# Weights of five attention groups of round two computed on VectorE during the first MoE

## The chip, the cores and the metric

One core of a Trainium2 chip runs the program. The metric is device time in microseconds (us) of one execution. The kernel before took 979.59 us, the median of three runs (979.09 to 980.57). Engines are written as in the profile: PE is TensorE (matrix products; PEld its loading of weights), DVE is VectorE, ACT is ScalarE, POOL is GpSimd, SP is SyncE; POOL and SP here issue transfers.

## The reference

An attention with pooled keys, whose output goes through a feed-forward layer (called MoE below). There are B = 4 batches with 12,288 queries each, C = 128 channels.

```python
kv_pool = kv.reshape(B, H // r, r, W // r, r, C).mean(axis=(2, 4))   # 768 keys a batch
kv_flat = kv_pool.reshape(B, -1, C) @ w_sr
k = v = kv_flat
s = scale * (q @ k.transpose(0, 2, 1))          # scale = 1 / sqrt(128)
a = np.exp(s - s.max(-1, keepdims=True))
a /= a.sum(-1, keepdims=True) + 1e-09
x = (a @ v).reshape(B * N, 128)
h = x @ w_in                                    # 128 -> 2048
g = h * (1.0 / (1.0 + np.exp(-1.702 * h)))
out = g @ w_out                                 # 2048 -> 128, fp32
```

The kernel takes the exponential without subtracting the maximum (the scores are small), and divides by the sum at the end.

## The kernel before

*Tiles.* The 49,152 queries are 96 groups of G = 512, 24 to a batch. For each group and each of JC = 6 chunks of 128 keys, TensorE makes a 128x512 tile of scores (L319), ScalarE its exponential into `ag` as bf16 (L321, three chunks an activation), and TensorE multiplies with the values: four query tiles of T = 128, for each a 128x129 product per chunk (L330); the 129th column of `v` is ones, so it is the sum. After three query tiles ("a unit") VectorE divides (L338, L346). In the MoE each group has FCH = 16 chunks: TensorE makes 128x512 of h (L433), ScalarE the activation into `ag` (L435), TensorE adds up the 16 products with w_out (L440), VectorE transposes the sum (L447), SP sends it out (L450).

*Rounds.* There are R = 2 rounds of 48 groups: attention of groups 0 to 47, MoE of 0 to 47, attention of 48 to 95, MoE of 48 to 95. `x` holds the attention output of one round. For the first 72 query tiles of a round it is turned on TensorE (`turn`, L356, L358), for the others by transfers through DRAM (L366, L372) during the MoE. Batches 2 and 3, which round two needs, are pooled during the first MoE: the sums by accumulating transfers (L161), then `use_kv`: sum on VectorE (L167), transposition (L172, L174), keys (L180, L181), values (L187, L189).

*Fills and drains.* A matmul that feeds an activation (L319, L433) is called a fill, one that uses its result (L330, L440) a drain. `ag` is one tile with AG = 108 slots of a chunk each. `place` gives slots out in a ring, `slot_of` says which are taken, `room_ahead` how many are free ahead. Drains may lag fills by as much as the ring holds.

*PSUM.* There are eight banks. Fills go to banks 0 to 2 and 3 to 5 in turn, three chunks each, and so a fill waits for the activation two before. Banks 6 and 7 are accumulators for all else (`acc`): the sum of a MoE group (`o_of`), a unit of the attention (`av_of`), a turn, the pooled keys. `closes` and `free` hold when the planner thinks an accumulator is free again.

*The order.* The scheduler of the language is off (`manual_schedule`); the order of instructions on each engine is the order of the Python calls. A loop over the activations (`seq`) plans it: it calls `fill(n + 2)`, then puts in whatever TensorE still has time for by the planner's clock, `now` for TensorE and `end` for ScalarE, in units of about one 512-column matmul: first a turn, then one of the `extras` (pooled keys), else the next drain in `todo`, as long as it ends before `limit`, or the ring is nearly full (`room`). Constants such as FIXED, CHUNK, COST and EVACUATE are the planner's estimates. Nothing in the plan keeps account of VectorE, but for fixed allowances. When a group first appears in `seq`, `background` or `background_moe` issues transfers for later groups: `load_qT` (SP, L200), `cast_q` (POOL, L195), `add_kv`, `put_away`, `bring_back`.

Of the kernel before, what the change touches and what calls it, by code (L numbers as in the profile page):

```python
# [6 lines left out]

F32 = mybir.dt.float32
F32R = mybir.dt.float32r
BF = mybir.dt.bfloat16  # L10
AF = mybir.ActivationFunctionType
AX = mybir.AxisListType
ADD = mybir.AluOpType.add
MUL = mybir.AluOpType.mult
GE = mybir.AluOpType.is_ge
LE = mybir.AluOpType.is_le
EQ = mybir.AluOpType.is_equal


@with_exitstack  # L20
def kernel(
    ctx, tc, q, kv, w_sr, moe_w_in, moe_w_out, out,
):
    nc = tc.nc
# [5 lines left out]
    JC = J // 128  # L30
    d_ff = moe_w_in.shape[1]
    FCH = d_ff // 128
    scale = 1.0 / (C ** 0.5)
# [20 lines left out]

    R = 2
    XS = NS // R
    AG = 108

    cpool = ctx.enter_context(tc.tile_pool(name="const", bufs=1))
    xpool = ctx.enter_context(tc.tile_pool(name="x", bufs=1))  # L60
# [122 lines left out]
    def make_v(b, a):  # L183
        ps = acc()
        pT = pTs.pop((b, a))
        for k in range(K):
            nc.tensor.matmul(ps[:, k * C:(k + 1) * C], pT[:, k * 128:(k + 1) * 128], w_sr_sb,  # L187
                             start=True, stop=True)
        nc.vector.tensor_copy(vs[b][:, a * K:(a + 1) * K, 0:C], ps[:, :h].rearrange("p (k c) -> p k c", k=K))  # L189

    qTs = {}

# [90 lines left out]


    slot_of = {}
    head = 8 * JC

    def place(chunks):
        nonlocal head
        if chunks[0][0] == "a" and chunks[0][1] < 8:  # L290

            lo = [i * JC + jc for _, i, jc in chunks]
            slot_of.update(zip(chunks, lo))
            return ag[:, lo[0]:lo[-1] + 1:JC, :]
        if head + len(chunks) > AG:
            head = 0
        lo = head
        head += len(chunks)
        busy = set(slot_of.values())
        for c in chunks:  # L300
            assert lo not in busy
            slot_of[c] = lo
            lo += 1
        return ag[:, head - len(chunks):head, :]

    def room_ahead():
        busy = set(slot_of.values())
        return next((n for n in range(AG) if (head + n) % AG in busy), AG)

    def weights(c):  # L310
        return ag[:, slot_of[c], :]


# [9 lines left out]
    def drain_attn(t, a):  # L323

        i, u, k = t // 4, t // TS, t % TS
        if k == a == 0:
            av_of[u] = acc(("av", u))
        o = t % 4 * T
        for jc in range(a * K, a * K + K):
            nc.tensor.matmul(av_of[u][:, k * (C + 1):(k + 1) * (C + 1)], weights(("a", i, jc))[:, o:o + T],  # L330
                             vs[i // GB][:, jc, 0:C + 1], start=(jc == 0), stop=(jc == JC - 1))
            if t % 4 == 3:
                del slot_of["a", i, jc]
        if k == TS - 1 and a == 1:
            close(("av", u), now + EVACUATE)
            ps = av_of.pop(u)[:, 0:TS * (C + 1)].rearrange("p (k c) -> p k c", k=TS)
            rec = npool.tile([128, TS], F32, name="rec")
            nc.vector.reciprocal(rec, ps[:, :, C])  # L338
            o = u * TS % (XS * SG // T)
            if o >= LATER:  # L340
                to = x[:, o * T:(o + TS) * T].rearrange("p (k c) -> p k c", k=TS)
            else:
                if u % 2 == 0:
                    xt_of[u // 2] = npool.tile([128, 2 * TS, C], BF, name="xt")
                to = xt_of[u // 2][:, u % 2 * TS:u % 2 * TS + TS, :]
            nc.vector.tensor_tensor(to, ps[:, :, 0:C], rec.unsqueeze(2).broadcast_to([128, TS, C]), MUL)  # L346
            if u % 2 and o < LATER:
                turns.append((now + TURN, u // 2))

    def turn(w):  # L350

# [56 lines left out]
    def background_moe(g):  # L408

        n, g = divmod(g, 4 * XS)  # L410
        m, odd = divmod(g - 9, 2)
        if 0 <= m < (4 * XS * G // T - LATER) // PART:
            (bring_back if odd else put_away)(n, m)
        g += n * 4 * XS
        for b, lo in ((2, 2), (3, 24)):
            if lo <= g < lo + 8:
                gate()
                add_kv(b, g - lo)
            if g in (lo + 10, lo + 12):
                use_kv(b, (g - lo - 10) // 2)  # L420

    def use_kv(b, a):
        sum_kv(b, a)
        extras.extend([(transpose_pooled, b, a), (make_k, b, a), (make_v, b, a)])

    extras = []
# [10 lines left out]
    def drain_moe(g, fc):  # L437
        if fc == 0:
            o_of[g] = acc(("o", g))
        nc.tensor.matmul(o_of[g], w_out_sb[:, fc, :], weights(("m", g, fc)),  # L440
                         start=(fc == 0), stop=(fc == FCH - 1))
        del slot_of["m", g, fc]
        if fc == FCH - 1:
            close(("o", g), now + EVACUATE)

            o_sb = opool.tile([128, 512], F32, name="o_sb")
            nc.vector.transpose(o_sb, o_of.pop(g))  # L447
            for m in range(4):
                eng = nc.scalar if g == NG - 1 and m % 2 else nc.sync
                eng.dma_start(out=out_r[g, m],  # L450
                              in_=o_sb[32 * m:32 * m + 32, :].rearrange("i (b j) -> i b j", j=32))
# [4 lines left out]
    chunks += [(i, jc) for jc in range(2) for i in range(4)]  # L456
    chunks += [(i, jc) for jc in range(2) for i in range(4, 8)]
    chunks += [(i, jc) for jc in range(2, JC) for i in range(8)]
    chunks += [(i, jc) for i in range(8, NG) for jc in range(JC)]
    seq, todo = [], []  # L460
    for n in range(R):
        part = chunks[n * NA // R:(n + 1) * NA // R]
        while part:
            m = sizes.pop(0) if sizes else K
            seq.append(("a", part[:m]))
            part = part[m:]
        todo += [("a", t, a) for t in range(n * NT // R, (n + 1) * NT // R) for a in range(2)]
        flat = [(g, fc) for g in range(n * NG // R, (n + 1) * NG // R) for fc in range(FCH)]
        todo += [("m",) + c for c in flat]
        for k in range(0, len(flat), K):  # L470
            seq.append(("m", flat[k:k + K]))

    at = {}
    for p, (kind, part) in enumerate(seq):
        for c in part:
            at[(kind,) + c] = p
    for kind, t, a in [k for k in todo if k[0] == "a"]:
        at["at", t, a] = max(at["a", t // 4, jc] for jc in range(a * K, a * K + K))

    begun = set()  # L480
# [1 line left out]
    def prepare(p):  # L482
# [10 lines left out]
        for i, _ in part:  # L493
# [25 lines left out]

    FIXED, CHUNK, SWITCH, HANDOVER, EVACUATE, LATE = 0.33, 1.975, 6.0, 1.0, 4.5, 1.0  # L520
    COST = {pool_chunk: (2.5, 2.0), key_chunk: (0.7, 2.0), value_chunk: (0.7, 2.0),
            transpose_q: (1.2, 4.0), key_and_value: (1.0, 3.0),
            transpose_pooled: (1.5, 3.0), make_k: (1.0, 3.0), make_v: (1.5, 3.0), turn: (1.5, 3.5)}
    SMALL, TURN = 0.27, 5.5
    PAUSE = 4.0
    now, end, extra_at = 0.0, [], 0.0
    done = 0

    def fill(p):
        nonlocal now  # L530
# [16 lines left out]
    for n in range(len(seq)):  # L547
        fill(n + 2)
        while True:
            room = room_ahead()  # L550
            limit = end[-1] - K - HANDOVER if n + 3 < len(seq) else 1e9
            bank = free[next_acc()]
            f = None
            if turns and max(now, bank) >= turns[0][0]:
                f, args = turn, turns[0][1:]
            if f is None and extras and now >= max(extra_at, bank):
                f, *args = extras[0]
            if f and max(now, bank) + COST[f][0] > limit + (LATE if f is turn else 4.5) and room >= 4 * K:
                f = None
            if f:  # L560
                now = max(now, bank) + COST[f][0]
                f(*args)
                free[last_acc] = now + COST[f][1]
                extra_at = now + PAUSE
                if f is turn:
                    turns.pop(0)
                else:
                    extras.pop(0)
                continue
            if done == len(todo):  # L570
                break
            kind, i, c = todo[done]
            needs = at[("at" if kind == "a" else kind, i, c)]
            cost = K * SMALL if kind == "a" else 1.0
            if needs > n or (kind == "a" and i % TS == c == 0 and at["at", i + TS - 1, 1] > n):
                break
            start = max(now, end[needs] + HANDOVER)
            if c == 0 and (kind == "m" or i % TS == 0):
                start = max(start, bank)
            if start + cost > limit and not (room < 2 * K + 1 or (room < 4 * K and start == now)):  # L580
                break
            now = start + cost
            (drain_attn if kind == "a" else drain_moe)(i, c)
            done += 1
    assert done == len(todo) and not turns and not extras


# [28 lines left out]
```

## Time and profile before

The profiled execution has a span of 977.3 us, from the first to the last instruction, and a time of 979.09 us, the lowest of the three runs; the granted TensorE clock is 0.998 on average.

| group (line, engine, operation) | count | busy us | mean ns |
|---|---|---|---|
| L433 PE, MoE fill, 512 columns | 1536 | 414.5 | 378 |
| L440 PE, MoE drain, 512 columns | 1536 | 410.8 | 379 |
| L319 PE, attention fill, 512 columns | 576 | 155.8 | 378 |
| L330 PE, attention drain, 129 columns | 2304 | 169.2 | 220 |
| L356 PE, turn, 128 columns | 144 | 11.9 | 218 |
| L435 ACT, MoE activation, 128x1536 | 512 | 689.9 | 1538 |
| L321 ACT, Exp, 128x1536 (+2 forms) | 196 | 260.3 | 1455 |
| L447 DVE, output transposition | 96 | 68.8 | 716 |
| L346 DVE, division, to `x` and to `xt` | 80 + 48 | 44.6 + 26.7 | 557 |

How to read it. Successive matmuls overlap, and so do successive activations: the mean duration is longer than the distance of their starts, and busy shares near 100% don't tell whether an engine could take more. Counts of instructions in a stretch, and starts in the timeline, do. The busy tenths over the span, in 40 slices of 24.4 us:

```profile
PE   7899999999999999999999999999999999999997
PEld 3567777544444444444457777754444444444443
DVE  4444333212110110201114433311101101001010
ACT  4999999999999999999999999999999999999997
```

Where PEld shows 7 is attention (up to 147 us, and 494 to 625 us), where it shows 4 is MoE. VectorE has least to do in the two MoEs.

### The profile page before, as it was taken

How to read it: one execution, taken by the hardware profiler on the slowest of the kernel's cores; microseconds unless marked ns; L12 is line 12 of the kernel's file. 1: busy time of each engine (PE TensorE's matmuls, PEld its weight loads, DVE VectorE, ACT ScalarE, POOL GpSimd, SP SyncE). 2: the span in 40 equal slices, each digit the busy share in tenths (PEclk: the TensorE clock that was granted, in tenths of full speed). 3: DMA queues.
4: the chain of work that ended last, by engine and by line, in shares of the span. 5: the costliest groups of instructions: out<-in, count | busy, mean ns of one | idle time of the engine just before them, and what ended most of it. 6: DMA issues, size and time to landing. Idle time of an engine off the chain costs nothing.

```text
span 977.3 us, 15763 instructions
## 1 busy us (share of the span) xinstructions
PE 960.9 (98%) x6431; PEld 511.9 (52%) x6431; DVE 207.7 (21%) x506; ACT 955.9 (98%) x713; POOL 65.5 (7%) x113
## 2 busy tenths in 40 slices
PE   7899999999999999999999999999999999999997
PEld 3567777544444444444457777754444444444443
DVE  4444333212110110201114433311101101001010
ACT  4999999999999999999999999999999999999997
POOL 3100101330000340000000000000000000000000
PEclk9999999999999999999999999999999999999999
DMA  9898851999672996222274531012566622222222
GB/s 181 165 195 151 110 89 35 122 154 167 129 140 44 138 160 79 33 44 41 36 129 88 105 70 23 1 22 40 117 125 120 116 44 33 43 34 38 39 33 44
DMA packets 335688, 84.99 MB, mean 87 GB/s; under 512 B 309568, under 2 KB 333248, under 8 KB 335296
## 3 DMA queue, kind: packets, MB, share of 16 engines
q1 hardware_dynamic: 305456, 51.34, 30.6%
q0 software_dynamic: 29104, 32.51, 21.8%
q8 instruction: 50, 0.82, 0.3%
q10 hardware_dynamic: 1056, 0.13, 0.1%
q14 instruction: 22, 0.18, 0.1%
HBM read 52.49 MB, written 43.52 MB: 98 GB/s over the span
## 4 chain that ended last, share of the span: by engine, by line
PE 76%; ACT 21%; issue 1%; DVE 1%; DMA 1%; POOL 0%; POOLq 0%
PE banks L433 24%; PE banks L440 24%; ACT ag L435 19%; PE banks L330 14%; PE banks L319 12%; ACT ag L321 1%; PE banks L356 1%; DVE qT L224 1%; DMA x<-in_kv_dram 1%; PE banks L129 0%; PE banks L218 0%; PE banks L265 0%; DVE pooled L167 0%; DVE xt L346 0%; PE banks L172 0%
## 5 line engine op out<-in xcount | busy, mean ns | idle before, releaser
L435 ACT ACTIVATE ag<-banks 128x1536 bf16<-128x1536 f32 x512 | 689.9, 1538 | 0.3 <-PE banks L433 0.2
L433 PE MATMUL banks<-x,w_in_sb 128*128 128x512 bf16 x1536 | 414.5, 378 | 0.2 <-ACT ag L435 0.2
L440 PE MATMUL banks<-ag,w_out_sb 128*128 128x512 bf16 x1536 | 410.8, 379 | 0.5 <-ACT ag L435 0.5
L321 ACT ACTIVATE ag<-banks 128x1536 bf16<-128x1536 f32 (+2 forms) x196 | 260.3, 1455 | 11.3 <-PE banks L319 10.8
L440 PEld LDWEIGHTS <-w_out_sb 128*128 128x128 bf16 x1536 | 149.5, 98 | 179.9 <-issue 1.0
L433 PEld LDWEIGHTS <-w_in_sb 128*128 128x128 bf16 x1536 | 148.0, 97 | 179.7 <-issue 23.0
L447 DVE STREAM_TRANSPOSE o_sb<-banks 128x512 f32<-128x512 f32 x96 | 68.8, 716 | 562.6 <-PE banks L440 562.6
L330 PEld LDWEIGHTS <-ag 128*128 128x128 bf16 x2304 | 150.4, 97 | 48.6 <-issue 1.5
L330 PE MATMUL banks<-v,ag 128*128 128x129 bf16 x2304 | 169.2, 220 | 0.7 <-DVE v L153 0.7
L319 PE MATMUL banks<-qT,kT 128*128 128x512 bf16 x576 | 155.8, 378 | 5.6 <-ACT ag L321 4.5
L319 PEld LDWEIGHTS <-kT 128*128 128x128 bf16 x576 | 48.9, 97 | 33.6 <-issue 4.0
L338 DVE RECIPROCAL rec<-banks 128x3 f32<-128x3 f32 x128 | 23.0, 180 | 133.5 <-PE banks L330 133.5
L346 DVE TENSOR_TENSOR x<-banks,rec 128x384 bf16<-128x384 f32 x80 | 44.6, 557 | 2.8
L161 POOL DMA_DIRECT2D kvs<-in_kv_dram x32 | 40.2, 1306 | 25.0 <-DMA kvs<-in_kv_dram 22.6
L380 POOL MEMSET gate_tile<- 1x8 f32 x38 | 3.6, 94 | 461.1 <-DVE gate_tile L379 461.1
L346 DVE TENSOR_TENSOR xt<-banks,rec 128x384 bf16<-128x384 f32 x48 | 26.7, 557 | 1.7
L358 DVE COPY x<-banks 128x768 bf16<-128x768 bf16 x24 | 13.4, 557 | 23.2 <-PE banks L356 23.2
L356 PE MATMUL banks<-ident,xt 128*128 128x128 bf16 x144 | 11.9, 218 | 0.0
L224 DVE COPY qT<-banks 128x512 bf16<-128x512 bf16 x15 | 9.8, 687 | 4.5 <-PE banks L218 4.4
L195 POOL DMA_DIRECT2D q_bf<-in_q_dram x20 | 9.9, 496 | 5.5 <-DMA x<-in_q_dram 2.1
L356 PEld LDWEIGHTS <-xt 128*128 128x128 bf16 x144 | 9.2, 97 | 0.9
L218 PE MATMUL banks<-ident,x 128*128 128x128 bf16 x64 | 5.9, 219 | 2.1 <-DVE qT L224 1.9
(56 smaller groups left out, 86.1 us busy)
## 6 DMA issues: line engine op xcount, KB each, us to landing
out_dram<-o_sb SPq DMA_DIRECT2D x382, 64.0 KB, 2.0
kvs<-in_kv_dram POOLq DMA_DIRECT2D x32, 384.0 KB, 6.3
q_bf<-in_q_dram POOLq DMA_DIRECT2D x20, 512.0 KB, 6.5
x_bf<-x SPq DMA_DIRECT2D x12, 640.0 KB, 4.6
x<-in_kv_dram POOLq DMA_DIRECT2D x12, 512.0 KB, 12.4
x<-in_q_dram POOLq DMA_DIRECT2D x3, 512.0 KB, 20.5
w_in_sb<-in_moe_w_in_dram POOLq DMA_DIRECT2D x1, 512.0 KB, 5.1
w_out_sb<-in_moe_w_out_dram POOLq DMA_DIRECT2D x1, 512.0 KB, 7.6
```

The source lines that it names most:

```text
L161: nc.gpsimd.dma_start(out=kv_sums[b][:, i2], in_=kv_p[b, i, w, :, i2], **({"accum_op": ADD} if n else {}))
L224: nc.vector.tensor_copy(dst, src)
L319: nc.tensor.matmul(ps[:, k, :], kTs[i // GB][:, jc * 128:(jc + 1) * 128], rhs, start=True, stop=True)
L321: nc.scalar.activation(place([("a",) + c for c in chunks]), ps, AF.Exp, scale=scale)
L330: nc.tensor.matmul(av_of[u][:, k * (C + 1):(k + 1) * (C + 1)], weights(("a", i, jc))[:, o:o + T], vs[i // GB][:, jc, 0:C + 1], start=(jc = ...
L338: nc.vector.reciprocal(rec, ps[:, :, C])
L346: nc.vector.tensor_tensor(to, ps[:, :, 0:C], rec.unsqueeze(2).broadcast_to([128, TS, C]), MUL)
L356: nc.tensor.transpose(ps[:, k, :], xt[:, k, :], ident)
L433: nc.tensor.matmul(ps[:, k, :], w_in_sb[:, fc * 128:(fc + 1) * 128], x[:, g % (4 * XS) * G:(g % (4 * XS) + 1) * G], start=True, stop=True)
L435: nc.scalar.activation(place([("m",) + c for c in chunks]), ps, AF.Gelu_apprx_sigmoid)
L440: nc.tensor.matmul(o_of[g], w_out_sb[:, fc, :], weights(("m", g, fc)), start=(fc == 0), stop=(fc == FCH - 1))
L447: nc.vector.transpose(o_sb, o_of.pop(g))
```

## The change

The exponentials of five groups, 48 to 52 (EARLY = 5, 30 chunks, ten activations of ScalarE), are taken out of round two's attention and are made on VectorE, during the first MoE. For each of the 30 chunks TensorE makes the scores into an accumulator (`early_fill`), and VectorE computes exp by ten operations on 128x512 fp32 (`early_exp`): scale by log2(e), clamp, round to an integer by adding 1.5 x 2^23, build 2^n from the integer's bits, and multiply by a polynomial of degree five in the rest. The result goes to one of 30 slots at the start of `ag`, which the ring leaves to them from group 12 of the first MoE on (`low`). AG falls from 108 to 102.

The planner gets a second list of drains, `todo_early`, from which it takes a whole unit of the attention when its chunks are made and no other group is half done; it may be as early as the first MoE. It also gets a clock for VectorE (`dve`, `on_dve`), by which it times the ten steps one at a time, the start of the next chunk, the return of accumulators after a division or an output transposition, and the pooled keys of batches 2 and 3. `background` for groups 48 and 52, which loads and casts q for later groups, is called at groups 40 and 46 of the first MoE.

```diff
-    AG = 108
+    EARLY = 5
+    AG = 102
...
-    head = 8 * JC
+    head, low = 8 * JC, 0
...
-            head = 0
+            head = low
...
+    early = range(NG // R, NG // R + EARLY)
+
     def weights(c):
+        if c[0] == "a" and c[1] in early:
+            return ag[:, (c[1] - early[0]) * JC + c[2], :]
         return ag[:, slot_of[c], :]
...
         if k == TS - 1 and a == 1:
-            close(("av", u), now + EVACUATE)
+            close(("av", u), max(now, dve - 1.0) + EVACUATE)
+            on_dve(4.3)
...
+    LN2 = 0.6931471805599453
+    MAGIC = 1.5 * 2.0 ** 23
+    COEFFS = (1.0000001192092896, -0.6931469440460205, 0.24022120237350464, -0.05550713464617729, 0.009675541892647743, -0.001327647129073739)
+
+    def early_fill(i, jc):
+        nonlocal steps
+        ps = acc()
+        rhs = qTs[i // 4][:, 0, (i % 4) * G:(i % 4 + 1) * G]
+        nc.tensor.matmul(ps, kTs[i // GB][:, jc * 128:(jc + 1) * 128], rhs, start=True, stop=True)
+        steps = early_exp(ps, weights(("a", i, jc)))
+        early_step()
+
+    def early_step():
+        nonlocal steps
+        on_dve(next(steps))
+        if steps.gi_frame.f_locals["last"]:
+            steps = None
+            made.add(early_todo.pop(0))
+
+    def early_exp(ps, out):
+        last = False
+        a = npool.tile([128, 512], F32, name="ea", bufs=1)
+        b = npool.tile([128, 512], F32, name="eb", bufs=1)
+        e = npool.tile([128, 512], I32, name="ee", bufs=1)
+        nc.vector.tensor_scalar(a, ps, scale / LN2, -126.0, MUL, MAX)
+        yield 3.5
+        nc.vector.tensor_scalar(b, a, 127.0, MAGIC, MIN, ADD)
+        yield 2.2
+        nc.vector.tensor_scalar(e, b, MAGIC - 127.0, 2.0 ** 23, SUB, MUL)
+        yield 2.2
+        nc.vector.scalar_tensor_tensor(b, b, MAGIC, a, SUB, SUB)
+        yield 3.5
+        nc.vector.tensor_scalar_mul(a, b, COEFFS[5])
+        yield 2.2
+        for k in (4, 3, 2, 1):
+            nc.vector.scalar_tensor_tensor(a, a, COEFFS[k], b, ADD, MUL)
+            yield 3.5
+        nc.vector.scalar_tensor_tensor(out, a, COEFFS[0], e.bitcast(F32), ADD, MUL)
+        last = True
+        yield 3.5
...
+        if g == 12:
+            low = EARLY * JC
+            head = max(head, low)
+        if g in (40, 46):
+            i = early[0] + 4 * (g // 46)
+            begun.add(("a", i))
+            background(i)
...
     def use_kv(b, a):
+        nonlocal extra_at
         sum_kv(b, a)
+        on_dve(3.5)
+        extra_at = max(extra_at, dve + 1.5)
...
-            close(("o", g), now + EVACUATE)
+            close(("o", g), max(now, dve - 1.0) + EVACUATE)
+            on_dve(3.6)
...
-    chunks += [(i, jc) for i in range(8, NG) for jc in range(JC)]
+    chunks += [(i, jc) for i in range(8, NG) for jc in range(JC) if i not in early]
...
+    def on_dve(cost):
+        nonlocal dve
+        dve = max(dve, now + 1.0) + cost
...
+            if steps and dve <= now + 2.0:
+                early_step()
+            if not f and not steps and early_todo and low and min(slot_of.values()) >= low and (2, 1) in vs and dve <= now + 2.0 and now >= bank:
+                f, args = early_fill, early_todo[0]
-            if f and max(now, bank) + COST[f][0] > limit + (LATE if f is turn else 4.5) and room >= 4 * K:
+            if f and max(now, bank) + COST[f][0] > limit + (LATE if f is turn else 0.0 if f is early_fill else 4.5) and room >= 4 * K:
                 f = None
...
+            if not source:
+
+                if todo_early and all((i, jc) in made for t in range(todo_early[0][1], todo_early[0][1] + TS)
+                                      for i in [t // 4] for jc in range(JC)):
+                    source = todo_early
+                else:
+                    source = todo
```

More of the change, by code (lines that the diff above doesn't have):

```diff
@@ L9 @@
 F32R = mybir.dt.float32r
+I32 = mybir.dt.int32
 BF = mybir.dt.bfloat16
@@ L16 @@
 LE = mybir.AluOpType.is_le
+SUB = mybir.AluOpType.subtract
+MAX = mybir.AluOpType.max
+MIN = mybir.AluOpType.min
 EQ = mybir.AluOpType.is_equal
@@ L189, in make_v @@
         nc.vector.tensor_copy(vs[b][:, a * K:(a + 1) * K, 0:C], ps[:, :h].rearrange("p (k c) -> p k c", k=K))
+        vs[b, a] = True
     qTs = {}
@@ L307, in room_ahead @@
         busy = set(slot_of.values())
-        return next((n for n in range(AG) if (head + n) % AG in busy), AG)
+        return next((n for n in range(AG - low) if (head - low + n) % (AG - low) + low in busy), AG - low)
+    early = range(NG // R, NG // R + EARLY)
     def weights(c):
+        if c[0] == "a" and c[1] in early:
+            return ag[:, (c[1] - early[0]) * JC + c[2], :]
         return ag[:, slot_of[c], :]
@@ L331, in drain_attn @@
                              vs[i // GB][:, jc, 0:C + 1], start=(jc == 0), stop=(jc == JC - 1))
-            if t % 4 == 3:
+            if t % 4 == 3 and i not in early:
                 del slot_of["a", i, jc]
         if k == TS - 1 and a == 1:
-            close(("av", u), now + EVACUATE)
+            close(("av", u), max(now, dve - 1.0) + EVACUATE)
+            on_dve(4.3)
             ps = av_of.pop(u)[:, 0:TS * (C + 1)].rearrange("p (k c) -> p k c", k=TS)
@@ L348, in drain_attn @@
                 turns.append((now + TURN, u // 2))
+    LN2 = 0.6931471805599453
[35 more added lines that the diff above has]
+        yield 3.5
+    made = set()
+    steps, early_todo = None, [(i, jc) for i in early for jc in range(JC)]
     def turn(w):
@@ L414, in background_moe @@
         g += n * 4 * XS
+        nonlocal head, low
+        if g == 12:
[5 more added lines that the diff above has]
+            background(i)
         for b, lo in ((2, 2), (3, 24)):
@@ L458 @@
     chunks += [(i, jc) for jc in range(2, JC) for i in range(8)]
-    chunks += [(i, jc) for i in range(8, NG) for jc in range(JC)]
+    chunks += [(i, jc) for i in range(8, NG) for jc in range(JC) if i not in early]
     seq, todo = [], []
+    todo_early = [("a", t, a) for t in range(NT) for a in range(2) if (t // TS * TS + TS - 1) // 4 in early]
     for n in range(R):
-        part = chunks[n * NA // R:(n + 1) * NA // R]
+        part = [c for c in chunks if c[0] // (NG // R) == n]
         while part:
@@ L466 @@
             part = part[m:]
-        todo += [("a", t, a) for t in range(n * NT // R, (n + 1) * NT // R) for a in range(2)]
+        todo += [("a", t, a) for t in range(n * NT // R, (n + 1) * NT // R) for a in range(2)
+                 if (t // TS * TS + TS - 1) // 4 not in early]
         flat = [(g, fc) for g in range(n * NG // R, (n + 1) * NG // R) for fc in range(FCH)]
@@ L476 @@
             at[(kind,) + c] = p
-    for kind, t, a in [k for k in todo if k[0] == "a"]:
+    for i in early:
+        for jc in range(JC):
+            at["a", i, jc] = at["a", early[-1] + 1, 0] - 1
+    for kind, t, a in [k for k in todo + todo_early if k[0] == "a"]:
         at["at", t, a] = max(at["a", t // 4, jc] for jc in range(a * K, a * K + K))
@@ L521 @@
     COST = {pool_chunk: (2.5, 2.0), key_chunk: (0.7, 2.0), value_chunk: (0.7, 2.0),
-            transpose_q: (1.2, 4.0), key_and_value: (1.0, 3.0),
+            transpose_q: (1.2, 4.0), early_fill: (1.0, 5.5), key_and_value: (1.0, 3.0),
             transpose_pooled: (1.5, 3.0), make_k: (1.0, 3.0), make_v: (1.5, 3.0), turn: (1.5, 3.5)}
@@ L526 @@
     now, end, extra_at = 0.0, [], 0.0
-    done = 0
+    source, dve = None, 0.0
+    def on_dve(cost):
+        nonlocal dve
+        dve = max(dve, now + 1.0) + cost
     def fill(p):
@@ L562 @@
                 f(*args)
-                free[last_acc] = now + COST[f][1]
-                extra_at = now + PAUSE
+                free[last_acc] = dve + 1.0 if f is early_fill else now + COST[f][1]
+                if f in (transpose_pooled, make_k, make_v):
+                    on_dve(2.5)
+                extra_at = max(now + PAUSE, dve + 1.5 if f in (transpose_pooled, make_k, make_v) else 0.0)
                 if f is turn:
                     turns.pop(0)
+                elif f is early_fill:
+                    pass
                 else:
@@ L569 @@
                 continue
-            if done == len(todo):
+            if not source:
[4 more added lines that the diff above has]
+                    source = todo
+            if not source:
                 break
-            kind, i, c = todo[done]
+            kind, i, c = source[0]
             needs = at[("at" if kind == "a" else kind, i, c)]
             cost = K * SMALL if kind == "a" else 1.0
-            if needs > n or (kind == "a" and i % TS == c == 0 and at["at", i + TS - 1, 1] > n):
+            first_of = c == 0 and (kind == "m" or i % TS == 0)
+            if source is not todo_early and (needs > n or (kind == "a" and first_of and at["at", i + TS - 1, 1] > n)
+                                             or (kind == "a" and i // 4 in early and (i // 4, JC - 1) not in made)):
+                if first_of:
+                    source = None
                 break
-            start = max(now, end[needs] + HANDOVER)
-            if c == 0 and (kind == "m" or i % TS == 0):
+            start = now if source is todo_early else max(now, end[needs] + HANDOVER)
+            if first_of:
                 start = max(start, bank)
             if start + cost > limit and not (room < 2 * K + 1 or (room < 4 * K and start == now)):
+                if first_of:
+                    source = None
                 break
@@ L583 @@
             (drain_attn if kind == "a" else drain_moe)(i, c)
-            done += 1
-    assert done == len(todo) and not turns and not extras
+            source.pop(0)
+            if not todo_early:
+                low = 0
+            if c == (1 if kind == "a" else FCH - 1) and (kind == "m" or i % TS == TS - 1):
+                source = None
+    assert not todo and not todo_early and not turns and not extras and not early_todo
 _INS = ['q', 'kv', 'w_sr', 'moe_w_in', 'moe_w_out']
```

## The prediction

> **What bounds the kernel now.** I read the totals first, then ScalarE's timeline, then TensorE's instruction counts by stretch, then its timeline in two places, then what waited for what, and last the groups on VectorE.
>
> ```profile
> PE 960.9 (98%) x6431; PEld 511.9 (52%) x6431; DVE 207.7 (21%) x506; ACT 955.9 (98%) x713; POOL 65.5 (7%) x113
> ```
>
> Two engines look full, so the question is which of them could go faster if the other did. ScalarE's timeline (start, length, instruction, count):
>
> ```profile
> 148.60 245.41 ACT L435 ACTIVATE ag<-banks 128x1536 bf16<-128x1536 f32 x182
> 494.21 1.28 ACT L321 ACT_TABLE_LOAD   x1
> 495.50 110.81 ACT L321 ACTIVATE ag<-banks 128x1536 bf16<-128x1536 f32 x82
> 625.43 1.28 ACT L435 ACT_TABLE_LOAD   x1
> 626.72 344.59 ACT L435 ACTIVATE ag<-banks 128x1536 bf16<-128x1536 f32 x256
> ```
>
> One activation of three chunks comes every 245.41/182 = 1.348 us in the first MoE, 110.81/82 = 1.351 in round two's attention, 344.59/256 = 1.346 in the second MoE. The stages begin at 147, 494 and 625 us. Now the counts of TensorE's instructions in four stretches of the two MoEs (the first "x" in each row):
>
> ```profile
> 270.00:370.00 100.00, 100.00 (x465) 45.34 (x464) 10.83 (x23) 100.00 (x75) 20.84 (x24) 1.00 0.85 121
> 660.00:760.00 100.00, 100.00 (x465) 45.35 (x464) 10.75 (x15) 100.00 (x75) 0.00 (x0) 1.00 0.53 100
> 820.00:870.00 50.00, 50.00 (x225) 21.64 (x224) 5.01 (x7) 50.00 (x38) 0.00 (x0) 1.00 0.24 37
> 870.00:920.00 50.00, 50.00 (x225) 21.57 (x224) 5.02 (x7) 50.00 (x39) 0.00 (x0) 1.00 0.24 37
> ```
>
> All four say 100% busy, but 465 matmuls go through in 100 us of the first two and 450 in the last two together. The timeline tells why; the starts of successive fills (L433) at 300 us, then at 821 us:
>
> ```profile
> 299.82 0.81 PE L433 MATMUL banks<-x,w_in_sb 128*128 128x512 bf16 x3
> 301.12 0.81 PE L433 MATMUL banks<-x,w_in_sb 128*128 128x512 bf16 x3
> 302.41 0.81 PE L433 MATMUL banks<-x,w_in_sb 128*128 128x512 bf16 x3
> ...
> 820.91 0.81 PE L433 MATMUL banks<-x,w_in_sb 128*128 128x512 bf16 x3
> 822.25 0.81 PE L433 MATMUL banks<-x,w_in_sb 128*128 128x512 bf16 x3
> 822.25 0.31 PEld L433 LDWEIGHTS <-w_in_sb 128*128 128x128 bf16 x2 [0.17 <-issue]
> ```
>
> At 300 us three fills and three drains (L440) take 1.295 us: 0.216 us each, none apart. At 821 us the same six take 1.344, so 0.049 us is idle. The first regime is TensorE's bound: ScalarE's 1.348 there is just 6.25 matmuls x 0.216, because a backlog of drains is being worked off. Only when it is gone, near 800 us, does TensorE have a hole in each activation. The waits count the holes (us in total, times, longest):
>
> ```profile
> PEld L433 <- issue: 23.0, 134, 0.5
> ```
>
> A second kind of hole stands at the pooled keys, here in the timeline, with the wait in brackets:
>
> ```profile
> 407.68 0.34 PE L172 MATMUL banks<-ident,pooled 96*128 96x96 bf16 x4 [0.30 <-DVE pooled L167]
> ```
>
> 134 holes of 0.049 = 6.6 us. Around the pooled keys of batches 2 and 3 (234 to 255 us, 391 to 415 us) the starts on TensorE leave 0.35 + 0.2 + 2 x 0.47 + 0.2 = 1.7 us. From 80 us to the last activation TensorE thus idles 8.3 us in all.
>
> **The change, part by part.** *ScalarE* loses 30 chunks, 10 activations: 10 x 1.35 = 13.5 us. That is the ceiling, and it is reached only if TensorE can deliver 13.5 us sooner. *TensorE* loses nothing: the 576 score matmuls become 546 + 30, the 2304 of the attention output and all others stay, by the instruction order of both programs. So its work is constant and the gain is what its idle time shrinks by, 8.3 us at most.
>
> I laid the order of the changed program beside the durations of before (0.216 for 512 columns, 0.059 for L330's 129, 0.055 for a transpose) and summed TensorE's issue time from mark to mark:
> - First MoE up to the 13th score chunk of round two: 28 more scores (6.0), 90 more attention matmuls (5.3), 12 more transposes (0.7), 26 fewer drains (-5.6), and smaller shifts: +6.6 us. TensorE had 1.7 us idle here, so this stage gets longer, by some 6.6 to 7.1.
> - Round two's attention, where TensorE has no gap: 82 activations left after that mark instead of 92, 125.0 us of matmuls become 112.2: -12.8. ScalarE needs 82 x 1.344 = 110.2 and is covered.
> - Second MoE up to its 240th activation: 319.0 become 325.2 (+6.2), which fills the 5.9 us of holes up to 950 us. The backlog, gone at activation 128 of this MoE before, is now gone at about 240 of 256, so 16 holes of 0.049 stay: 0.8.
>
> Sum with no other idle: 8.3 - 0.8 = 7.5 us off. From this the idle that the new order still has:
> - Batch 2's pooled keys, ahead of the first new matmul and in the same order: 0.6.
> - Batch 3's: the order puts two more drains before the first transposition, but VectorE is now busy. 0 to 0.9; 0.4.
> - Two extra turns in the first MoE (L412) wait for a normalisation that may stand behind a step of the polynomial: 0 to 0.9 each (a step of 0.7 us and a bit); 0.5 for both.
> - 30 scores, each in one of two accumulator banks that VectorE must have read before TensorE uses it again; behind a matmul that waits for it stand the next fill and drains, and ScalarE waits for those. At least 0; at most a whole step of 0.72 us each, 21.6. The nearest rows are the output groups, which hand the same banks back in about 1 us (0.72 of it the transpose), and the list of waits names none of TensorE for them: so near 0. One in ten hit by 0.2 us gives 0.6, with 0.1 of small holes 0.7.
> 7.5 - 0.6 - 0.4 - 0.5 - 0.7 = 5.3 us.
>
> *VectorE* gets ten operations of 128x512 fp32 for each chunk. Rows that price them:
>
> ```profile
> L181 DVE CAST kT<-banks 128x384 bf16<-128x384 f32 x4 | 2.2, 557 | 3.3 <-PE banks L180 3.3
> L152 DVE CAST kT<-banks 128x128 bf16<-128x128 f32 x6 | 1.7, 288 | 2.6 <-PE banks L151 2.6
> L167 DVE TENSOR_TENSOR pooled<-kvs 96x512 bf16<-96x512 f32 x4 | 2.6, 646 | 0.0
> L447 DVE STREAM_TRANSPOSE o_sb<-banks 128x512 f32<-128x512 f32 x96 | 68.8, 716 | 562.6 <-PE banks L440 562.6
> L273 DVE CAST wide<-ones 128x512 fp32r<-128x512 bf16 x1 | 0.5, 494 | 0.0
> ```
>
> From 128 to 384 columns out of PSUM costs (557 - 288)/256 = 1.05 ns a column, so 512 cost 0.69. The one read of PSUM and the six of two tensors: 0.646 to 0.716, taken 0.69. The three with one SBUF tensor: nearest is the cast to 512 four-byte words, 0.49; ends 0.42 (the 219 ns of the 128-column L260 and 384 columns at half that slope) and 0.62. Ten dependent steps have 34 ns between them, as those at 1 us do. So 7 x 0.69 + 3 x 0.49 + 0.3 = 6.6 us a chunk, 6.1 to 7.2. The order places a score each 18 fills, six activations of some 1.35: 8.1 us, of which the output transposes need 6 x 3/16 x 0.716 = 0.81. Left: 7.3. It fits, even at 7.2, by 0.1. VectorE is then 91% busy in the first MoE, so an output transpose can stand up to 0.7 us behind a step of the polynomial; that is what the item on the banks holds.
>
> The Trainium skill, "VectorE: DVE Perf Modes", section "The TRN2 errata", gives a two-tensor fp32 operation (N+151)/0.96 GHz, 0.691 us here, and its tier table doubles the one-tensor ones: 0.42. By the page a chunk is 6.4 us; no row has these operations.
>
> The ring for weights shrinks from 108 to 102 slots, of which 30 are kept for VectorE in the first MoE: 72 turn. The order shows at most some 61 filled chunks undrained, and then forces drains ahead of fills; that is in the 6.6. Two transposing loads of q (L200) move up SP's queue, to groups 40 and 46 of the first MoE, past the output transfers of 10 and of 6 groups. The second overwrites q that the early scores read; in the order the last of these reads comes 17 activations (23 us) ahead, so SP should not stand and I price it at nothing. If it did stand, the outputs behind it would, and VectorE after three of them, for each group 7.2 us.
>
> A rule speaks against this whole account. The Trainium skill, "TensorE: Matmul & The Clock Gate", section "Back-to-back issue gap", gives 131 ns for a sustained 512-column matmul among weight loads. By it TensorE would be idle a third of the time and all 13.5 us would come. The 0.216 us at 300 us disagree, and the measurement decides.
>
> **Result.** The profiled execution has a span of 977.3 and a time of 979.09, 0.5 below the median of 979.59. 977.3 - 5.3 = 972.0 span, 973.8 time; I name 974.0 as between it and the median.
>
> **Rivals.** (1) *ScalarE alone is the bound:* 979.1 - 13.5 = 965.6. For it: ScalarE is 98% busy. Against: 465 matmuls in 100 us leave no room. 4%. (2) *VectorE hands banks back late:* each of 30 scores costs TensorE 0.2 us, 6 us, the gain is gone: about 979.8. Decides where chains take 7.3 us or more of the 8.1. For it: 0.1 us to spare at the upper bound. Against: the middle value spares 0.7. 8%. (3) *VectorE becomes the bound of the first MoE:* a step of 0.83 instead of 0.69, 8.3 a chunk: 30 x 1.0 = 30 late, less 5: about 1004. It is slower from 7.5 us a chunk on (0.18 x 30 = 5.3). Against: no row near 0.8 for 512 columns. 8%. (4) *The gain halves,* with 2 to 3 us more of bank and turn waits: 976.5. 15%. Forecast: 65%, with its own range 971.8 (all extra idle nil: 979.1 - 7.5, rounded up by what batch 2 keeps) to 976.
>
> 0.2% (2.0 us) is what a measurement can tell here. Faster by more: forecast, (1), (4) and part of (2), 0.85; within: 0.06; slower: 0.09. The range of 8 in 10: 971.6 to 978.
>
> **What would show it.** Before 950 us the TensorE counts are 465 per 100 us everywhere. The table load before round two's attention comes later, at 494.2 + 6.6 + (2.2 - 1.7 of idle) = 501.3, the one before the second MoE earlier, at 625.4 + 7.1 - 12.8 = 619.7. 186 activations with Exp, VectorE busy 208 + 198 = 406 us. Wrong if TensorE shows waits for VectorE of over 3 us in sum, if the holes stay after 800 us, or if the attention's table load moves earlier.

## The result, and the profile after

The changed kernel takes 975.15 us, the median of four runs (974.9 to 976.53), beside 980.08 (979.09 to 980.6) before: a ratio of 0.9954 with a 95% interval of 0.9937 to 0.9971. A second comparison of the same two kernels, on five new runs, gave 974.96 and 979.27, 0.9955 (0.9942 to 0.9967). So it is faster by 4.3 to 4.9 us; 974.0 was forecast.

The totals of the profile after:

```profile
PE 956.3 (98%) x6431; PEld 513.2 (53%) x6431; DVE 385.6 (40%) x806; ACT 945.0 (97%) x703; POOL 65.8 (7%) x113
```

TensorE executes the same 6431 matmuls, ScalarE ten activations less, and VectorE has nearly doubled. The counts by stretch late in the second MoE, in the columns of before (TensorE's count is the first "x"):

```profile
820.00:870.00 50.00, 50.00 (x233) 22.66 (x232) 5.73 (x8) 50.00 (x38) 0.00 (x0) 1.00 0.24 37
870.00:920.00 50.00, 50.00 (x233) 22.71 (x232) 5.02 (x7) 50.00 (x38) 0.00 (x0) 1.00 0.28 43
```

Where 225 matmuls went through in 50 us, 233 do now: the holes are gone. ScalarE's timeline shows where each stage begins (a load of the table) and where the longest new idle time stands:

```profile
431.29 48.80 ACT L502 ACTIVATE ag<-banks 128x1536 bf16<-128x1536 f32 x36 [2.46 <-PE banks L500]
...
503.48 1.28 ACT L331 ACT_TABLE_LOAD   x1
...
622.10 1.28 ACT L502 ACT_TABLE_LOAD   x1
```

The stages by these loads, in us. The first one begins later here, mostly because of a single wait, told below.

| | begins | first MoE | attention 2 | second MoE to the end | span |
|---|---|---|---|---|---|
| before | 147.3 | 346.9 | 131.2 | 351.9 | 977.3 |
| after | 149.0 | 354.5 | 118.6 | 352.6 | 974.7 |

Attention 2 gives 12.6 us, and the first MoE takes 7.6 of them back. The waits list of after, what remains on TensorE (us in total, times, longest):

```profile
PEld L500 <- issue: 3.7, 20, 0.3
...
PE banks L329 <- DMA qT<-q_bf: 1.3, 1, 1.3
PE banks L507 <- DVE v L194: 0.9, 2, 0.4
...
PE banks L412 <- DVE xt L357: 0.6, 1, 0.6
```

20 small holes are left of 134. The wait for q stands at 72.5 us, in the attention of round one, and not in every execution: the other three of this kernel have spans of 973.1 to 973.5. The waits for `v` (two) and for `xt` are new; here are the first for `v` and the one for `xt` in the timeline (start, length, engine, what; lines between are left out):

```profile
402.57 0.81 PE L500 MATMUL banks<-x,w_in_sb 128*128 128x512 bf16 x3
402.61 0.72 DVE L515 STREAM_TRANSPOSE o_sb<-banks 128x512 f32<-128x512 f32 x1 [0.28 <-PE banks L507]
403.25 0.52 DVE L194 CAST v<-banks 128x384 bf16<-128x384 f32 x1
403.82 1.24 PE L507 MATMUL banks<-ag,w_out_sb 128*128 128x512 bf16 x5 [0.43 <-DVE v L194]
```

```profile
427.11 1.21 PE L340 MATMUL banks<-v,ag 128*128 128x129 bf16 x18
428.16 0.38 PE L507 MATMUL banks<-ag,w_out_sb 128*128 128x512 bf16 x1
428.57 0.56 DVE L357 TENSOR_TENSOR xt<-banks,rec 128x384 bf16<-128x384 f32 x1
429.18 0.49 PE L412 MATMUL banks<-ident,xt 128*128 128x128 bf16 x6 [0.65 <-DVE xt L357]
```

In the first, the next drain was due at 402.57 + 3 x 0.216 = 403.22 and started at 403.82: 0.60 us lost, because the copy of the pooled values (L194), which holds the bank that the next output group wants, stands behind an output transposition. VectorE itself had been idle for 0.28 us before that transposition. In the second, a turn comes one drain (428.16) behind the attention unit whose division it depends on: the division ends at 429.13, and TensorE starts at 429.18 instead of 428.37, 0.81 us late.

VectorE's new groups (busy us, mean ns):

```profile
L397 DVE SCALAR_TENSOR_TENSOR ea<-ea,eb 128x512 f32<-128x512 f32 x120 | 82.3, 686 | 3.4
L386 DVE TENSOR_SCALAR ea<-banks 128x512 f32<-128x512 f32 x30 | 20.8, 692 | 33.1 <-PE banks L370 32.9
L394 DVE TENSOR_SCALAR ea<-eb 128x512 f32<-128x512 f32 x30 | 13.2, 440 | 0.9
```

With 418 and 435 for the other two steps of one tensor and 687 and 688 for the other two of two, a chunk costs 6.1 us and 9 x 0.034 between: 6.4.

### The profile page after: what moved, and what is told of

Its sections match the earlier page's. It is cut to its first block, busy times and chain, and to the rows that moved or that the text cites. A ratio compares the mean times of both kernels' runs of the same rounds, so it can differ in the third digit from the quotient of the medians.

```text
span 974.7 us, 16041 instructions
## 1 busy us (share of the span) xinstructions
PE 956.3 (98%) x6431; PEld 513.2 (53%) x6431; DVE 385.6 (40%) x806; ACT 945.0 (97%) x703; POOL 65.8 (7%) x113
## 4 chain that ended last, share of the span: by engine, by line
PE 91%; ACT 4%; DMA 3%; DVE 1%; issue 0%; POOL 0%; ACTq 0%; POOLq 0%
PE banks L500 33%; PE banks L507 33%; PE banks L340 13%; PE banks L329 11%; ACT ag L502 3%; DMA qT<-q_bf 2%; ACT ag L331 1%; DMA x<-in_q_dram 1%; PE banks L412 1%; PE banks L370 1%; DVE qT L230 1%; PE banks L224 0%; DVE o_sb L515 0%; PE banks L134 0%; DVE v L194 0%
## 5 line engine op out<-in xcount | busy, mean ns | idle before, releaser
L331 ACT ACTIVATE ag<-banks 128x1536 bf16<-128x1536 f32 (+1 forms) x186 | 247.4, 1466 | 13.2 <-PE banks L329 12.4
L329 PE MATMUL banks<-qT,kT 128*128 128x512 bf16 x546 | 147.8, 378 | 6.9 <-ACT ag L331 4.5
L397 DVE SCALAR_TENSOR_TENSOR ea<-ea,eb 128x512 f32<-128x512 f32 x120 | 82.3, 686 | 3.4
L329 PEld LDWEIGHTS <-kT 128*128 128x128 bf16 x546 | 46.7, 97 | 35.8 <-issue 4.0
L386 DVE TENSOR_SCALAR ea<-banks 128x512 f32<-128x512 f32 x30 | 20.8, 692 | 33.1 <-PE banks L370 32.9
L399 DVE SCALAR_TENSOR_TENSOR ag<-ea,ee 128x512 bf16<-128x512 f32 x30 | 20.6, 687 | 1.4
L392 DVE SCALAR_TENSOR_TENSOR eb<-eb,ea 128x512 f32<-128x512 f32 x30 | 20.6, 688 | 0.9
L394 DVE TENSOR_SCALAR ea<-eb 128x512 f32<-128x512 f32 x30 | 13.2, 440 | 0.9
```

What stands on the lines that cost most here:

```text
L329: nc.tensor.matmul(ps[:, k, :], kTs[i // GB][:, jc * 128:(jc + 1) * 128], rhs, start=True, stop=True)
L331: nc.scalar.activation(place([("a",) + c for c in chunks]), ps, AF.Exp, scale=scale)
L386: nc.vector.tensor_scalar(a, ps, scale / LN2, -126.0, MUL, MAX)
L397: nc.vector.scalar_tensor_tensor(a, a, COEFFS[k], b, ADD, MUL)
```

## The experiments

Each was compared with runs of the kernel before on the same chip. Stages are as in the table above.

| label | us | ratio to before (interval) | first MoE | attention 2 | second MoE |
|---|---|---|---|---|---|
| e1_two_steps | 975.21 | 0.9958 (0.9946 to 0.9971) | 354.5 | 118.6 | 352.6 |
| e5_clock | 977.84 | 0.9986 (0.9977 to 0.9995) | 352.1 | 123.7 | 352.6 |
| e2_act_480 | 975.38 | 0.9955 (0.9939 to 0.9972) | 353.8 | 118.8 | 352.6 |
| e3_m1_15 | 972.74 | 0.9927 (0.9910 to 0.9943) | 352.0 | 118.4 | 352.7 |
| e4_m2_15 | 973.56 | 0.9933 (0.9918 to 0.9948) | 354.5 | 118.6 | 351.3 |
| e8_plus4 | 1015.94 | 1.0370 (1.0351 to 1.0388) | 392.6 | 120.4 | 352.6 |
| f1_early0 | 986.03 | 1.0069 (1.0055 to 1.0082) | 346.4 | 138.2 | 351.9 |
| f2_early1 | 976.26 | 0.9967 (0.9955 to 0.9980) | 346.5 | 128.5 | 352.2 |
| e6_early2 | 973.85 | 0.9942 (0.9929 to 0.9956) | 346.1 | 125.7 | 352.7 |
| f3_early2 | 973.90 | 0.9949 (0.9936 to 0.9961) | 346.1 | 125.7 | 352.7 |
| e6_early3 | 975.45 | 0.9959 (0.9947 to 0.9972) | 350.6 | 123.0 | 352.5 |
| f4_early5 | 974.96 | 0.9955 (0.9942 to 0.9967) | 354.5 | 118.6 | 352.6 |

### Who is the bound: ScalarE shortened, TensorE shortened

```diff
-        nc.scalar.activation(place([("m",) + c for c in chunks]), ps, AF.Gelu_apprx_sigmoid)
+        to = place([("m",) + c for c in chunks])
+        n = 480 if chunks[0][0] < NG // R else 512
+        nc.scalar.activation(to[:, :, 0:n], ps[:, :, 0:n], AF.Gelu_apprx_sigmoid)
```

> The changed kernel, with the activations of the first MoE on 480 of each 512 columns (the last 32 keep what the slot held): ScalarE has 256 x 96 columns less, 256 x 0.083 = 21 us. Theory (TensorE has no gap in the first MoE): at most the few holes that ScalarE causes there go, 0.2 to 0.7 us: 974.5 to 975.2, ratio to before 0.995. Rival (ScalarE's time decides): 954.

Measured 975.38, 0.2 us above what the theory allowed. ScalarE's timeline from 247 us on:

```profile
246.92 68.87 ACT L504 ACTIVATE ag<-banks 128x1440 bf16<-128x1440 f32 x51 [1.87 <-PE banks L500]
```

68.87/51 = 1.350 us an activation, with a sixteenth of its columns gone: the distance is the one of before. ScalarE's time does not decide in the first MoE, which shrinks by 0.7 us of 354.5. It is also the answer to the page of the Trainium skill that gave 131 ns a matmul ("TensorE: Matmul & The Clock Gate", "Back-to-back issue gap"): with a sixteenth less for ScalarE to do, the matmuls came no closer than 0.214 to 0.216.

```diff
-        nc.tensor.matmul(o_of[g], w_out_sb[:, fc, :], weights(("m", g, fc)),
-                         start=(fc == 0), stop=(fc == FCH - 1))
+        short = g < NG // R        # e3; g >= NG // R in e4
+        if not (short and fc == FCH - 1):
+            nc.tensor.matmul(o_of[g], w_out_sb[:, fc, :], weights(("m", g, fc)),
+                             start=(fc == 0), stop=(fc == FCH - 1 - short))
```

> The changed kernel with 15 of the 16 drains of each group in the first MoE (the last 128 of d_ff are left out of the sum there): 48 matmuls of 0.216 us less, 10.4 us. Theory: TensorE is the bound from group 13 on (35 x 0.216 = 7.6), and ScalarE's own pace stands closely behind before that (1 us of 2.8): 966 to 967.5. Rival (ScalarE's time decides): no change, 975.

> The changed kernel with 15 of the 16 drains of each group in the second MoE: again 10.4 us of TensorE less. Theory: in this stage TensorE's 1.349 us an activation stand only just above ScalarE's 1.343, so 256 x 0.006 = 1.4 us come and no more: 973.5 to 974. Rival (TensorE alone decides in all stages): 965.

e4 came as expected: 973.56, the second MoE 1.4 us shorter (352.65 to 351.28) and nothing else. e3 did not: 972.74, where 966 to 967.5 was expected; the first MoE gave 2.5 us and not 8. The distances of the starts of every 16 activations in the first MoE, in us, taken from the traces, tell why:

```
after: 21.31 21.64 21.58 21.68 23.39 21.46 21.58 21.77 21.50 22.48 21.57 22.27 25.64 21.63 22.04
e3:    21.31 21.63 21.29 21.62 23.07 21.38 21.44 21.66 21.39 22.34 21.55 21.82 25.15 21.63 21.78
```

A stretch is three groups, so three drains less are 0.65 us of TensorE. Most stretches of after stand at 21.3 to 21.8. Without a drain a group they come to 21.3 to 21.7, near ScalarE's 16 x 1.330 to 1.343 = 21.3 to 21.5: the ten of them give 0.8 us of 6.5, so ScalarE's own pace stands 0 to 0.3 us behind TensorE's in them. The length that the stage has gained lies in five lumps (23.39, 22.48, 22.27, 25.64, 22.04), where more of TensorE's work goes through between two activations: eleven drains at once at 247 us in the first, pooled keys or the attention of an early unit, some with its turn, in the others. These five give the other 1.7 us, of 3.2. So TensorE is the bound, but in most of the stage only by one per cent, and an even saving on it is soon ScalarE's.

The first lump comes soon after group 12, where the ring gives up 30 of its slots, and drains have to go ahead of fills when it is full. With two groups (below), where it gives up 12, the same stretch takes 21.38 us. The ring was not varied by itself.

### What the idle time that is left comes from

```diff
-        nc.vector.tensor_scalar(b, a, 127.0, MAGIC, MIN, ADD)
...
-        nc.vector.scalar_tensor_tensor(out, a, COEFFS[0], e.bitcast(F32), ADD, MUL)
+        for cost in (2.2, 2.2, 3.5, 2.2, 3.5, 3.5, 3.5, 3.5):
+            yield cost
+        nc.vector.tensor_copy(out, a)
```

> The changed kernel with eight of the ten VectorE steps of each early chunk left out (the scaled scores are copied as weights; no exponential for those 30 chunks), in the same order on TensorE. Theory A (what idle TensorE has left comes from the places in its own order: the drain right behind make_v, the turn right behind a division; VectorE stood idle just before both): only the two 0.2 us waits after early scores go, 974.7 against 975.2, ratio to before 0.9948 to 0.9955. Rival B (VectorE's load causes the 2.6 us that TensorE waits between 360 and 460 us): 972.5, ratio 0.9926 or less.

Measured 975.21, and all stages are those of after to 0.1 us. TensorE's waits in its profile:

```profile
PE banks L496 <- DVE v L194: 0.9, 2, 0.4
...
PE banks L401 <- DVE xt L357: 0.6, 1, 0.6
```

The same waits, with VectorE all but relieved of the polynomial. They come from the places in TensorE's order, as theory A had it. The two waits of 0.2 us after early scores, which it expected to go with the load, are still there (0.23 and 0.21 us by the starts).

```diff
-                turns.append((now + TURN, u // 2))
+                turns.append((now + TURN + (6.0 if i in early else 0.0), u // 2))
...
-                free[last_acc] = dve + 1.0 if f is early_fill else now + COST[f][1]
                 if f in (transpose_pooled, make_k, make_v):
                     on_dve(2.5)
+                late = f in (early_fill, make_v) and last_acc not in closes
+                free[last_acc] = dve + 1.0 if late else now + COST[f][1]
```

> The changed kernel with two corrections of the planner: the accumulator of the pooled values counts as free only when VectorE's clock says so, and the turns of early groups come 6 units (1.3 us) later. All work is kept. Theory A: the waits of 2 x 0.6 us at the pooled values and 0.8 + 0.2 at the turns go, 2.0 us: 973.2, ratio to before 0.9934. Rival B (VectorE's load): waits move to other places, 975.2, ratio 0.995.

Measured 977.84, slower than the change. The first MoE did give what was expected, 354.5 to 352.1, and both waits for `v` are gone. But attention 2 grew by 5.1 us. Its timeline there:

```profile
527.33 0.69 DVE L399 SCALAR_TENSOR_TENSOR ag<-ea,ee 128x512 bf16<-128x512 f32 x1
528.14 0.81 PE L329 MATMUL banks<-qT,kT 128*128 128x512 bf16 x3 [0.54 <-ACT ag L331]
...
530.13 3.48 PE L340 MATMUL banks<-v,ag 128*128 128x129 bf16 x57
```

The last early chunk is now ready at 528 us only, 28 us after the table load that begins this stage; in after it is 21 us. The planner draws the attention of group 52 first and had no other drain to put in: four fills with TensorE idle between them, then 57 drains at once, for which ScalarE waits 5.6 us. A repair of two microseconds in one stage moved a due time in the next. Which of the two corrections moved it, and whether they would keep their 2 us with another order of drains, was not tried.

### How much VectorE can take

```diff
         nc.vector.tensor_scalar_mul(a, b, COEFFS[5])
+        for k in range(4):
+            nc.vector.scalar_tensor_tensor(e, e, 0.0, e, MUL, ADD)
```

> The changed kernel with four more two-tensor steps (e = e x 0 + e, which leaves e as it is) in each early chunk: 6.4 + 4 x 0.72 = 9.3 us of VectorE a chunk, the order unchanged. Chunks come 8.95 us apart in the mean and 8.0 where they stand closest, and 0.89 of it is the output transposes'. Theory: VectorE has 8.06 us a chunk, so it falls behind by 1.2 us on each of 30 and TensorE waits for its banks: some 35 us slower than the change, 1005 to 1012. Rival (VectorE has time enough): 975 to 978.

Measured 1015.94, 41 us slower than the change where 30 to 37 was expected; the first MoE alone takes 38.1 more, 1.27 us a chunk instead of 1.24. The counts in the first MoE:

```profile
270.00:370.00 100.00, 89.55 (x417) 40.75 (x424) 94.64 (x158) 89.64 (x66) 12.80 (x15) 1.00 0.62 97
```

VectorE is 95% busy, TensorE and ScalarE 90%. So the rival that VectorE becomes the bound is a real one, it begins between 6.4 us a chunk and 9.3, and the change stays clear of it.

### How many groups

```diff
-    EARLY = 5
+    EARLY = 3        # and 2, 1, 0
```

With EARLY = 0 the two loads of q keep their groups 48 and 52 (`NG // R` stands for `early[0]`, which is empty then).

> EARLY = 3 instead of 5: 18 chunks, six activations taken from ScalarE instead of ten. Theory (TensorE's issue time is fixed, the gain is the idle time that goes; six activations are 8.1 us, about as much as the 8.3 us of idle): 974.5 to 976, as with five. Rival 1 (ScalarE's time decides, 1.35 us an activation): 5.4 us behind five, 980.5. Rival 2 (each activation brings its share of the measured 4.9): 977.1.

> EARLY = 2: 12 chunks, four activations (5.4 us) taken from ScalarE. Theory: TensorE's issue time up to the second MoE is 600.5 us in this order, against 600.3 with five groups, and ScalarE's 348 activations at 1.343 from 147 us on plus two table loads are 470 against TensorE's 471, so about the same: 974.5 to 976.5. Rival 1: 8.1 us behind five groups, 983. Rival 2: 978.1.

> EARLY = 1: six chunks, two activations, 2.7 us of ScalarE. Theory: TensorE reaches the second MoE with 604.2 us of work done instead of 606.5, the holes of 0.049 us then begin at activation 174 instead of 128, and the 0.9 us at the pooled keys of batch 3 go: 2.3 + 0.9 = 3.2 less, but no more than ScalarE's 2.7: 976.5 to 977.5.

> EARLY = 2 once more, beside the change itself on one chip: 973.7 to 974.5 if the 0.1% between them is real, 975.2 if not.

> The change itself once more: 975 to 975.5, ratio to before 0.995.

> EARLY = 0: nothing is computed ahead, but the planner's clock for VectorE, the ring of 102 slots and the earlier loads of q stay. TensorE's issue time at every mark is that of before, within 0.2 us. Theory: 979.3 to 980.2, as before. Rival (the planner's clock or the order of the loads brings part of the gain): 977 to 978.

Three groups bring what five do (975.45), and two at least as much: 973.85, 0.65 below the range expected, and 973.9 beside 974.96 for five on the same chip, with intervals that overlap. ScalarE has four activations less there instead of ten. One group gives 976.26, a little faster than the 976.5 that ScalarE's share was to allow. From two groups on neither a price per activation (977 to 978) nor ScalarE's time (980 to 983 for fewer than five) fits. Up to two, though, the gain is what ScalarE loses: 2.7 us for two activations, where 3.0 was measured, and 5.4 for four, where 5.4 was.

What fits all of them is a fixed sum on TensorE. Its small holes, with one, two and five groups (134 before, 46 with three):

```profile
PEld L500 <- issue: 15.8, 90, 0.4
PEld L500 <- issue: 5.8, 30, 0.4
PEld L500 <- issue: 3.7, 20, 0.3
```

With the longer waits, the starts from 160 us to the last MoE group leave TensorE idle for about 8.2 us before and 5.2, 2.2, 4.1 and 3.7 us with one, two, three and five groups (a few matmuls are missing from the records; a gap of just one matmul was not taken as idle). That is 3.0, 6.0, 4.1 and 4.5 us less idle time, beside gains of 3.0, 5.4, 3.8 and 4.3 us. Three and five groups bring waits of 0.4 to 0.8 us at pooled keys and turns; with one and two no wait there is over 0.25 us.

The stages show the same: each group taken from attention 2 shortens that stage by some 2.2 to 2.8 us, and up to two groups the first MoE does not grow. With the third it grows by 4.5 us where attention 2 shrinks by 2.7, and with two more by 3.9 where it shrinks by 4.4.

With EARLY = 1 and 2 the ring takes the early slots back while query tile 195, or tiles 198 and 199, are still to read them: these tiles are weighed with other chunks' values, everything else is computed as before, and the instructions are the same. So their times show what the order costs; a kernel with two groups that keeps its slots until the last reader was not run.

EARLY = 0 was expected to change nothing and cost 6.8 us. Its timeline after the first MoE:

```profile
504.29 1.66 SPq L206 DMA_TRANSPOSE qT<-q_bf  x1
506.05 7.27 SPq L518 DMA_DIRECT2D out_dram<-o_sb  x11
509.86 0.72 DVE L515 STREAM_TRANSPOSE o_sb<-banks 128x512 f32<-128x512 f32 x1 [15.21 <-DMA out_dram<-o_sb]
510.63 1.13 PE L340 MATMUL banks<-v,ag 128*128 128x129 bf16 x9 [4.64 <-DVE o_sb L515]
```

The load of q that moved to group 46 overwrites what groups 48 to 51 read. With none of them early, those reads come in attention 2, and SP stands at this load with eleven output transfers behind it. The three output buffers are full, VectorE waits 15.2 us for one, and TensorE for VectorE. With five groups the load goes out at 489.4 us, and costs nothing on TensorE, though the two output transfers just before it land 6.3 to 6.5 us after their issue instead of 2. So it is this edit that depends on the early groups. The planner's clock for VectorE brings at most half a microsecond by itself up to there (the first MoE of EARLY = 0 takes 346.4 us beside 346.9); what it would bring in attention 2 can't be seen behind the stand.

## Why the prediction was right, point by point

- *The bound.* Right: TensorE's sum is fixed, and the gain is its idle time. e2 shows it from ScalarE's side, the number of groups from the other. What it did not say is how close ScalarE stands behind: e3 showed 0 to 0.3 us in 21.5 over most of the first MoE, and up to two groups the gain is ScalarE's time.
- *The ceiling of 8.3 us and the holes.* Right. The starts on TensorE leave 0.8 us of holes in the last activations, as forecast.
- *Stage by stage.* First MoE +6.6 to 7.1 forecast, +7.6 measured; attention 2 -12.8 and -12.6; second MoE +0.3 (6.2 of added work less 5.9 of holes) and +0.7.
- *The idle of the new order.* 2.2 us forecast, 3.0 measured by the starts between 200 and 640 us: batch 2's keys 0.6 and 0.16; batch 3's 0.4 and 1.2; the turns 0.5 and 0.97; early scores waiting for their banks 0.7 and 0.44; and 0.2 at the start of the second MoE, not foreseen. So 8.3 - 0.8 - 3.0 = 4.5 us instead of 5.3, and 4.3 to 4.9 were measured. That the sum is off by only 0.8 is partly luck: batch 2's keys and the scores came 0.7 below their terms, batch 3's keys, the turns and the unforeseen wait 1.5 above.
- *The term that was mis-sized* is batch 3's keys: "the order puts two more drains before the first transposition, but VectorE is now busy. 0 to 0.9; 0.4." The transposition did go free, as the two drains promised; but the copy of the values holds a bank that the next group wants, 0.6 us twice. And the reason was wrong for it and for the turns: not VectorE's load (e1), but that the planner counts a bank as free, and a turn as due, by its own clock.
- *VectorE.* 6.6 us a chunk forecast, 6.4 measured, busy 406 and 385.6. The Trainium skill's page "VectorE: DVE Perf Modes", section "The TRN2 errata", with its (N+151)/0.96, and the section "The perf-mode tier table", with twice the rate for one fp32 tensor in SBUF, had given an estimate of 6.4. The trace has 686 ns for its 691 and 418 to 440 for its 424, so for the steps of one tensor it was nearer than the 0.49 that I took from a row. The scores come 8.95 us apart in the mean, not 8.1, which I had from the closest ones; that leaves more room than I gave.
- *SP.* Priced at nothing, rightly, with the reason that was given: f1 shows the stand that the early reads prevent.
- *The rivals.* (1) falls by e2 and by the number of groups. (2) and (3) did not come; e8 shows that (3) exists and has about the size that its sum gives (1.27 us late a chunk for 1.24). (4), at half the gain, was close: the profiled pair alone differs by only 2.6 us, because that execution of the changed kernel lost 1.7 us in its first 80, most of it at the wait for q.

## What to carry to other kernels

When two engines both look full, count instructions per stretch and compare the distances of their starts: the one whose distance is the sum of its own work is the bound, and taking work from the other gains no more than the holes on the first. Then ask for the least change that fills the holes; here three groups did what five do, and the order with two was as fast. And a plan with a clock for each engine has to give back each buffer by the clock of the engine that reads it last, and repairs to it have to be measured to the end: one that saved 2.4 us in one stage cost 5.1 in the next.

## What was not expected of the hardware

- ScalarE's activations of 1536 columns start 1.330 us apart in many places of both traces, and 1.342 to 1.345 in the second MoE of before from 820 us on, where TensorE has its holes, though each lasts 1.44 to 1.73 us in the record: they overlap, and the length of one doesn't give the rate.
- VectorE at 79% from 250 to 500 us, nearly always on fp32 operands, slowed neither TensorE nor ScalarE that could be seen: with eight of ten steps left out (e1) every stage kept its length to 0.1 us. The step that reads PSUM stayed in e1, so its share was not tested.
